# A gated-delta attention and SwiGLU kernel: chunk 0's K, its norms, its first scores, the first up products and the last stores cut into halves, with a new order of the whole program

## The chip, the cores and the metric

The kernel runs on one core of one Trainium2 chip. The metric is the device time of one execution in microseconds; a kernel's time is the median of its runs. TensorE is PE in the profile (its weight loads PEld), VectorE is DVE, ScalarE ACT, GpSimd POOL, and SyncE, whose queue issues nearly all DMAs, SP.

## The reference

Two stages follow each other, all in float32. The first is a delta rule over 768 steps for 4 batches and 8 heads of 48 columns. The second is a SwiGLU layer with RMS norm over the 3072 tokens, 384 columns wide and 1536 inside.

```python
k_n = k / (np.linalg.norm(k, axis=-1, keepdims=True) + 1e-06)
for t in range(S):
    kt, vt, bt = (k_n[:, :, t], v[:, :, t], beta[:, :, t, None])
    y[:, :, t] = np.einsum('bhd,bhde->bhe', q[:, :, t], state)
    v_old = np.einsum('bhde,bhd->bhe', state, kt)
    state = state + bt[:, :, :, None] * np.einsum('bhd,bhe->bhde', kt, vt - v_old)
...
rms = np.sqrt(np.mean(x * x, axis=-1, keepdims=True) + 1e-06)
xn = x / rms * rms_g
g = xn @ w_gate
silu = g * (1.0 / (1.0 + np.exp(-g)))
val = xn @ w_val
return (silu * val @ w_out).astype(np.float32)
```

Here x is y with the heads side by side, one row of 384 for each token.

## The kernel before

The 768 steps are cut into 12 chunks of 64 (`C`). In a chunk the recurrence becomes matrix work: the scores of K with K, the inverse of a unit triangular 64x64 matrix for each of 32 batch-heads, products of that inverse with V less what the state holds, scores of Q with K, and an update of the state. The 256 tokens of a chunk (4 batches of 64, kept as two token halves of 128) then go through the RMS norm and the feed-forward part.

Each chunk passes these stages:

- `load` reads K, Q and V; for chunk 0 K comes in two DMAs of 192 KB, one on SP's queue and one on ACT's. `norms` squares K on ACT (L711), sums on DVE (L712) and takes the root on POOL (L715). `turn` transposes K and Q on PE (L659) for the first chunks; later K goes through DRAM.
- `prep` makes the inverse. `scores` (L690) gives K with K, ACT scales it (L919), four DMAs store it to DRAM (`dkk`) and two read it back with the batch-heads on the partitions (`at`). DVE multiplies by beta (L938) and makes shares (L965, L975, L970), for chunks below 4; above, POOL does so. Then 15 steps of a product and a sum on DVE (L987, L993) build the inverse of 32x32 blocks. It goes out to DRAM (`dx`) and back into `mt` and `x2bd`, and three small products (L1044 or a DMA, L1068, L1092) merge the blocks to 64x64.
- `prep_first` does this for chunk 0 without DRAM: 16x16 blocks are copied out of the scores (L775, L777), turned on DVE (L779), scaled by the norms (L797, L800), run through 7 steps (L829, L835) and copied to `mtb` (L864, L866). A product with the rest of the scores gives `gmb` (L879, copies L889 and L891), and `recur` for chunk 0 applies it three times (L1225, L1240, copies L1254).
- `recur` otherwise takes the state into account (L1131, L1143), applies the inverse (L1192, copies L1277 and L1279), multiplies with the Q scores (L1206) and updates the state (L1291). For x it then squares on ACT (L1315), takes the mean on DVE (L1322) and the root on POOL (L1327), scales on ACT (L1333), transposes on PE (L1358) and multiplies by g (L1363 on DVE, L1367 on ACT).
- `ffn_plain` does the feed-forward part of chunks 0 and 1: up products of 128x256 (L1430), Silu (L1437), product (L1438), down products of 128x384 (L1412), first for six of the twelve blocks f of 128 inner columns, later for the rest. `ffn` does chunks 2 to 11 with fewer products: 15 instead of 18 for a half (L1523) and 7 instead of 8 in `down` (L1581, sums L1590).
- `weights` loads and converts the 18 weight tiles of 768 KB (ACT L617 and L618, DVE L619 and L620), which arrive as 64-bit floats in pairs of words.

No engine order is written out by hand. All operations go into a `Plan` with durations, priorities (`due`, `rush`) and dependencies. `settle` plans forward and backward `ROUNDS` times, and each number in `MOVES` seeds one further change that is replayed when the program is built (`vary`, `attempt`). The resulting order of each engine's instructions and of SP's DMAs is fixed. Up to a planned time `WARM`, `filler` puts products with the identity (L1701) into PE's planned gaps. Each engine runs its instructions in that order and waits for semaphores; SP uses eight DMA semaphores in turn.

The pieces that the change and the prediction touch are `load`, `turn`, `norms`, `prep_first`, the `fast` test in `prep`, the multiplication by g in `recur`, `up` in `ffn_plain`, and `add` and `store` in `down`. The stores of a chunk's result stand behind its last sums:

```python
def store(p):
    for bb in range(2):
        tok = (2 * bb + p) * S + c * C
        dma(out[tok : tok + C, :], o_sb[p][64 * bb : 64 * bb + 64], -1, ...)
```

## Time and profile before

| | us |
|---|---|
| median of 3 runs | 679.27 |
| the runs | 679.56, 673.34, 679.27 |
| the profiled execution | 678.64 |
| its span, first to last instruction | 676.3 |
| PE busy | 658.9 |
| DVE busy | 535.4 |
| ACT busy | 314.3 |
| POOL busy | 118.8 |
| mean granted PE clock | 0.997 |

A row of busy time by stretches has the stretch, its length, then for PE, PEld, DVE, ACT and POOL the busy time and in brackets the number of instructions, then PE's granted clock, the DMA share and GB/s. A row of the chain has start, length, and what the end waited for. A row of the timeline has start, length, engine, line, operation, output and inputs with sizes, the count, and in brackets the engine's idle time before it with what ended that. A float32 product of the program is two records of the trace.

### The profile page before, as it was taken

The numbers are of one execution on the slowest core, as the hardware profiler recorded it, in microseconds if no ns is written. First come the engines' busy times: TensorE is split into PE (matmuls) and PEld (weight loads), VectorE is DVE, ScalarE is ACT, GpSimd is POOL, SyncE is SP. The second block draws the span as 40 slices with busy tenths as digits, with TensorE's granted clock in tenths as the row PEclk, the third lists the DMA queues.
The fourth block names the chain that finished last, engine by engine and source line by source line (L and its number), as shares of the span: only waits on it lengthen the run. The fifth ranks groups of instructions, "written<-read, shape, count | busy, mean of one in ns | idle before, by whom it ended". The sixth has DMA issues, their size and how long they took to land.

```text
span 676.3 us, 23308 instructions
## 1 busy us (share of the span) xinstructions
PE 658.9 (97%) x9896; PEld 608.1 (90%) x9896; DVE 535.4 (79%) x1142; ACT 314.3 (46%) x763; POOL 118.8 (18%) x95
## 2 busy tenths in 40 slices
PE   8889989999998999999999999999999999999997
...
GB/s 95 155 257 80 191 205 143 270 90 128 92 121 125 43 75 121 104 66 135 82 74 116 84 103 119 97 44 106 122 46 91 102 75 48 25 57 2 25 1 23
DMA packets 285976, 66.61 MB, mean 98 GB/s; under 512 B 269104, under 2 KB 276784, under 8 KB 285872
## 3 DMA queue, kind: packets, MB, share of 16 engines
q1 hardware_dynamic: 284832, 64.93, 53.0%
q8 instruction: 77, 1.26, 0.8%
...
## 4 chain that ended last, share of the span: by engine, by line
PE 79%; DVE 8%; DMA 6%; SPq 4%; issue 1%; ACT 1%; POOL 0%; DVEq 0%
PE bank L1523 37%; PE bank L1581 21%; PE bank L1430 5%; SPq L509 4%; PE bank L690 3%; PE bank L1412 2%; DVE acc L993 2%; DMA at<-dkk 2%; PE bank L1206 2%; DVE acc L987 2%; DMA q<-in_q_dram 2%; PE bank L1092 1%; PE bank L1143 1%; PE bank L1192 1%; PE bank L1131 1%
## 5 line engine op out<-in xcount | busy, mean ns | idle before, releaser
L1523 PE MATMUL bank<-xf,w_in 128*128 128x128 f32 x1440 | 179.8, 277 | 0.0
L1523 PEld LDWEIGHTS bank<-xf,w_in 128*128 128x128 f32 x1440 | 170.0, 192 | 1.6 <-issue 0.8
L1534 DVE TENSOR_TENSOR tmp<-tmp,bank 128x512 f32<-128x512 f32 x180 | 120.7, 681 | 43.6 <-PE bank L1523 37.7
L1523 PE MATMUL bank<-xf,more 128*128 128x128 f32 x960 | 124.2, 277 | 0.0
L1523 PEld LDWEIGHTS bank<-xf,more 128*128 128x128 f32 x960 | 115.1, 192 | 1.3
L1536 ACT COPY tmp<-bank 128x512 f32<-128x512 f32 x120 | 69.6, 585 | 81.9 <-PE bank L1523 67.3
L1540 ACT ACTIVATE tmp<-tmp 128x256 f32<-128x256 f32 x120 | 49.7, 417 | 82.7 <-DVE tmp L1534 82.4
L993 DVE TENSOR_REDUCE acc<-acc 128x30 f32<-128x90 f32 (+4 forms) x165 | 78.0, 473 | 5.7
L1581 PE MATMUL bank<-wo_sb,hf 128*128 128x192 f32 x360 | 65.6, 333 | 0.6 <-DVE hf L1541 0.6
L938 POOL TENSOR_TENSOR at<-at,bs 128x1024 f32<-128x1024 f32 x8 | 18.9, 2360 | 246.9 <-DMA at<-dkk 148.1
L1581 PEld LDWEIGHTS bank<-wo_sb,hf 128*128 128x128 f32 x360 | 59.1, 193 | 2.1 <-DVE hf L1541 0.9
L987 DVE TENSOR_TENSOR acc<-acc,at 128x60 f32<-128x60 f32 (+4 forms) x165 | 56.4, 342 | 2.6
L1541 DVE TENSOR_TENSOR hf<-tmp 128x256 f32<-128x256 f32 x120 | 49.6, 429 | 10.4 <-ACT tmp L1540 9.2
L715 POOL TENSOR_TENSOR knrm<-ksum,half 128x16 f32<-128x16 f32 x12 | 35.7, 2971 | 88.3 <-DVE ksum L714 45.4
L1430 PE MATMUL bank<-xf,w_in 128*128 128x256 f32 x144 | 34.4, 385 | 0.3 <-DVE w_in L620 0.3
L1412 PE MATMUL bank<-wo_sb,hf 128*128 128x384 f32 x96 | 33.9, 493 | 0.0
L1430 PE MATMUL bank<-xp,w_in 128*128 128x256 f32 x144 | 33.1, 382 | 0.0
L1327 POOL TENSOR_TENSOR rs<-ms,mhalf 128x2 f32<-128x2 f32 (+1 forms) x13 | 9.7, 748 | 126.0 <-DVE ms L1322 85.6
L1430 PEld LDWEIGHTS bank<-xf,w_in 128*128 128x128 f32 x144 | 26.6, 190 | 5.6 <-DVE w_in L620 0.9
L1430 PEld LDWEIGHTS bank<-xp,w_in 128*128 128x128 f32 x144 | 27.0, 190 | 4.7 <-issue 0.2
L1590 DVE TENSOR_TENSOR tmp<-tmp,bank 128x192 f32<-128x192 f32 x30 | 10.5, 350 | 25.7 <-PE bank L1581 25.6
L1412 PEld LDWEIGHTS bank<-wo_sb,hf 128*128 128x128 f32 x96 | 17.8, 190 | 10.4 <-DVE hf L1438 0.6
...
## 6 DMA issues: line engine op xcount, KB each, us to landing
...
```

What stands on the lines that cost most here:

```text
L509: op = P.add(eng, dur, lambda: queue.dma_start(out=dst, in_=src), prio, r, w, lat=0.1)
L715: P.add("POOL", 2.95 if c < 2 else 3.3, lambda: nc.gpsimd.tensor_tensor(out=knrm[i2], in0=ksum[i2], in1=half, op=ALU.pow), pn, r=[("ksum", ...
L987: nc.vector.tensor_tensor(out=acc[:, 1:3, 0:n, j + 2 : W].rearrange("p a i t -> p i a t"), in0=acc[:, old, 0:n, j : j + 2, None].to_broadc ...
L993: nc.vector.tensor_reduce(out=acc[:, new, 0:n, j + 2 : W], in_=acc[:, lo : lo + 3, 0:n, j + 2 : W].rearrange("p a i t -> p i t a"), axis=A ...
L1412: nc.tensor.matmul(po[p].t[:, 0:DM], hf[:, spot(f), 128 * p : 128 * p + 128], wo_sb[:, spot(f)], start=(f == f0), stop=(f == f1 - 1), skip ...
L1430: nc.tensor.matmul(ps.t[:, TOK * side : TOK * side + TOK], w_in[:, side, h_, 3 * t + i_, n : n + 128], x_[:, 2 * t : 2 * t + 2].rearrange( ...
L1523: nc.tensor.matmul(g.t[:, 128 * z : 128 * z + 128], fac[:, side, 128 * f : 128 * f + 128], xf[:, xs], start=(begin and z == 0), stop=False ...
L1534: P.add("DVE", V(512), lambda t=t, g=g: nc.vector.tensor_tensor(out=t, in0=t, in1=g.t, op=ALU.add), -1, r=[g], w=[tk], last=g)
L1536: P.add("ACT", A(512), lambda t=t, g=g: nc.scalar.copy(t, g.t), -1, r=[g], w=[tk], last=g)
L1540: P.add("ACT", A(256), lambda t=t: nc.scalar.activation(out=t[:, 0:256], in_=t[:, 0:256], func=ACTF.Silu), -1, w=[tk])
L1541: P.add("DVE", V(256), lambda t=t, f0=f0, p=p: nc.vector.tensor_tensor(out=hf[:, spot(f0) : spot(f0) + 2, 128 * p : 128 * p + 128], in0=t[ ...
L1581: nc.tensor.matmul(g.t[:, 0:192], a_[:, f], b_[:, f], start=(begin and f == 0), stop=(f == 5), skip_group_check=True)
```

## The change

K of chunk 0 is loaded in four DMAs of 8 heads each, two on SP and two on ACT; its square, sum and turn work by such halves. The first scores are computed as 32x32 squares straight into two banks, and one copy for each bank replaces four. The up products of the first two blocks f are computed for 128 tokens at a time. For the last chunk each finished column half is stored at once, one DMA on SP and one on ACT. The scaling by beta and the shares go to POOL from chunk 2 on (`FASTC`), and all multiplications by g are done by ACT. The planner's constants, seed and list of moves are new, and the order of the instructions on every engine follows from them. The diff, with the lists of moves left out:

```diff
--- before.py
+++ after.py
@@ -22,42 +22,42 @@
 STRETCH = {"PE": 1.5, "ACT": 1.5, "DVE": 1.4, "POOL": 1.2, "SP": 1.0}
 ENGINES = ("PE", "ACT", "DVE", "POOL", "SP")
 OVERLAP = {"PE": 0.0, "ACT": 0.1, "DVE": 0.08, "POOL": 0.06, "SP": 0.0}
-ROUNDS, SEED = 24, 5
+ROUNDS, SEED = 24, 7
 MOVES = (
...
 )
-FETCH, AHEAD = 67.0, 160.0
+FETCH, AHEAD = 67.0, 120.0
 EARLY = 130.0
 FETCH0, AHEAD0 = 42.0, 130.0
-STICK = 2.0
+STICK = 0.5
 SHAKE = 0.06
 PATIENT = 0.3
 RING, LANES, FIRST, LAND = 2330, 8, 1.08, 0.9
-WARM = 60.0
-CLEAR = (0.3, 0.6, 0.9)
+FASTC = 2
+WARM = 56.0
+CLEAR = (0.2, 0.5, 0.8)
 TURNK = range(4, 12)
 BEGIN = 1.7
-ONSET = {"PE": 1.0, "ACT": 2.6, "DVE": 0.85, "POOL": 0.35, "SP": 0.5}
+ONSET = {"PE": 1.0, "ACT": 3.2, "DVE": 0.85, "POOL": 0.35, "SP": 0.5}
 TILE = 1.5
 EARLYM = 0.4
-MARGIN = 1.4
+MARGIN = 1.0
 TURNX = range(2, 11)
-DUE0 = 44.0
-DUE1 = 70.0
-DUE2 = 156.0
+DUE0 = 50.0
+DUE1 = 82.0
+DUE2 = 154.0
 PERIOD = 51.0
 W1 = 26.0
-CV2 = 75.0
-FAC = 105.0
+CV2 = 65.0
+FAC = 95.0
 TAIL0 = 20.0
-RUSH = 25.0
-RUSHW = 0.0
+RUSH = 35.0
+RUSHW = 10.0
 RUSH1 = 10.0
 RUSHC = 5.0
 
@@ -298,7 +298,7 @@
 
         rng = random.Random(n)
         kind, keys = rng.random(), list(keys)
-        a = rng.choice((rng.uniform(0.0, 650.0), rng.uniform(0.0, 220.0)))
+        a = rng.choice((rng.uniform(0.0, 650.0), rng.uniform(0.0, 220.0), rng.uniform(0.0, 110.0), rng.uniform(0.0, 110.0)))
         if kind < 0.25:
             w, s = rng.choice((10.0, 30.0, 80.0)), rng.choice((0.5, 2.0, 6.0))
             keys = [k + rng.gauss(0.0, s) if a < t < a + w else k for k, t in zip(keys, starts)]
@@ -638,9 +638,15 @@
             for g in range(2):
                 if key[0] not in what or key == "q2" and c > 1:
                     continue
+                if key == "k2" and c == 0:
+                    for hv in range(2):
+                        dst = t[64 * g : 64 * g + 64, 8 * hv : 8 * hv + 8, 0:D]
+                        s = src.rearrange("b (y g) t e -> g t (b y) e", g=2)[g, t0 : t0 + C, 8 * hv : 8 * hv + 8]
+                        dma(dst, s, pr + 0.1 * hv, w=[("k2", 0, g) if hv else ("k2h", g)], dur=0.7, work=0.75, desc=512, eng="ACT" if g else "SP")
+                    continue
                 dst = t[64 * g : 64 * g + 64, :, 0:D]
                 s = src.rearrange("b (y g) t e -> g t (b y) e", g=2)[g, t0 : t0 + C]
-                dma(dst, s, pr, w=[(key, c % NK, g)] if key == "k2" else q2k[8 * g : 8 * g + 8], dur=0.7, work=1.5 if c < 3 else 1.15, desc=1024, eng="ACT" if c == 0 and g and key == "k2" else "SP", bulk=c > 0 or key == "q2")
+                dma(dst, s, pr, w=[(key, c % NK, g)] + [("k2h", g)] * (c % NK == 0) if key == "k2" else q2k[8 * g : 8 * g + 8], dur=0.7, work=1.5 if c < 3 else 1.15, desc=1024, eng="ACT" if c == 0 and g and key == "k2" else "SP", bulk=c > 0 or key == "q2")
         if "v" in what:
             for g in range(2 if c == 0 else 0):
                 s = v.rearrange("b (y g) t e -> g t (b y) e", g=2)[g, t0 : t0 + C]
@@ -662,7 +668,7 @@
                         ident,
                     )
 
-            P.add("PE", 0.55, tr, pr, r=r + ["ident"], w=[ps, keys[hv]], ps=ps, size=8)
+            P.add("PE", 0.55, tr, pr, r=(r if isinstance(r, list) else r[hv]) + ["ident"], w=[ps, keys[hv]], ps=ps, size=8)
             if dst is qt:
                 out_ = dst[:, 4 * hv : 4 * hv + 4]
                 src_ = lambda ps=ps: ps.t.rearrange("p (u t) -> p u t", u=4)
@@ -701,17 +707,22 @@
         return [("kt", i, hv) for hv in range(2)] + [("ktr", i, n) for n in range(4)]
 
     def kkeys_(c):
-        return [("k2", c % NK, 0), ("k2", c % NK, 1)]
+        return [("k2", c % NK, 0), ("k2", c % NK, 1)] + [("k2h", 0), ("k2h", 1)] * (c == 0)
 
     def norms(c):
         i2 = c % 2
         pn = ((1.0, 8.0)[c] if c < 2 else due(c, 130))
         kd = k2[c % NK][:, :, 0:D]
 
-        P.add("ACT", A(768), lambda: nc.scalar.square(r_, kd), pn, r=kkeys_(c), w=[("r", 0), ("r", 1)])
-        P.add("DVE", V(768), lambda: nc.vector.tensor_reduce(out=ksum[i2], in_=r_, axis=AXL.X, op=ALU.add), pn, r=[("r", 0), ("r", 1)], w=[("ksum", i2)], lat=0.05)
-
-        P.add("DVE", 0.17, lambda: nc.vector.tensor_scalar_max(ksum[i2], ksum[i2], 1e-30), pn, w=[("ksum", i2)])
+        for hv in range(2 if c == 0 else 1):
+            x_ = slice(8 * hv, 8 * hv + 8) if c == 0 else slice(0, 16)
+            n = 384 if c == 0 else 768
+            rk, ks = ([("r", hv)], ("ks", hv)) if c == 0 else ([("r", 0), ("r", 1)], ("ksum", i2))
+            kk_ = [("k2", 0, g) if hv else ("k2h", g) for g in range(2)] if c == 0 else kkeys_(c)
+            P.add("ACT", A(n), lambda x_=x_: nc.scalar.square(r_[:, x_], kd[:, x_]), pn, r=kk_, w=rk)
+            P.add("DVE", V(n), lambda x_=x_: nc.vector.tensor_reduce(out=ksum[i2][:, x_], in_=r_[:, x_], axis=AXL.X, op=ALU.add), pn, r=rk, w=[ks], lat=0.05)
+
+        P.add("DVE", 0.17, lambda: nc.vector.tensor_scalar_max(ksum[i2], ksum[i2], 1e-30), pn, r=[("ks", 0), ("ks", 1)] if c == 0 else [], w=[("ksum", i2)])
         P.add("POOL", 2.95 if c < 2 else 3.3, lambda: nc.gpsimd.tensor_tensor(out=knrm[i2], in0=ksum[i2], in1=half, op=ALU.pow), pn, r=[("ksum", i2), "half"], w=[("knrm", i2)])
 
         def inv():
@@ -764,18 +775,29 @@
 
     def prep_first():
         kn, ktk, kkeys = k2[0], ktkeys(0), kkeys_(0)
-        turn(kn, kt[0], ktk, kkeys + [("k2p", 0)], 0.0, True)
-        ps = scores(kt[0], kt[0], 0.0, ktk, [])
-        for q_ in range(4):
-            rows, cols = slice(W * q_, W * q_ + W), slice(W * (q_ % 2), W * (q_ % 2) + W)
-            for d in range(2):
-                dst = sq1[rows].rearrange("p (x n) -> p x n", n=W)[:, d:16:2]
-                src = lambda d=d, rows=rows, cols=cols, ps=ps: heads(ps[d])[rows, :, cols]
-                if d:
-                    P.add("DVE", 0.45, lambda dst=dst, f=src: nc.vector.tensor_copy(out=dst, in_=f()), 0.0, r=[ps[d]], w=[("sq1", q_, d)], last=ps[d])
-                else:
-                    P.add("ACT", A(256), lambda dst=dst, f=src: nc.scalar.copy(dst, f()), 0.0, r=[ps[d]], w=[("sq1", q_, d)], last=ps[d])
-        sqk = [("sq1", q_, d) for q_ in range(4) for d in range(2)]
+        turn(kn, kt[0], ktk, ([("k2h", 0), ("k2h", 1), ("k2p", 0)], [("k2", 0, 0), ("k2", 0, 1), ("k2p", 0)]), 0.0, True)
+        pq = [Group(), Group()]
+
+        def squares():
+            for u in range(8):
+                for th in range(2):
+                    for d in range(2):
+                        for g in range(2):
+                            side = kt[0][64 * d : 64 * d + D, g, u, W * th : W * th + W]
+                            r0, n = 64 * g + W * th, W * u
+                            nc.tensor.matmul(pq[d].t[r0 : r0 + W, n : n + W], side, side)
+
+        P.rows = 32
+        P.add("PE", 1.7, squares, 0.0, r=ktk, w=pq, ps=pq, size=256)
+        P.rows = 128
+        for d in range(2):
+            dst = sq1.rearrange("p (x n) -> p x n", n=W)[:, d:16:2]
+            src = lambda d=d: pq[d].t[:, 0:256].rearrange("p (u n) -> p u n", n=W)
+            if d:
+                P.add("DVE", V(256), lambda dst=dst, f=src: nc.vector.tensor_copy(out=dst, in_=f()), 0.0, r=[pq[d]], w=[("sq1", d)], last=pq[d])
+            else:
+                P.add("ACT", A(256), lambda dst=dst, f=src: nc.scalar.copy(dst, f()), 0.0, r=[pq[d]], w=[("sq1", d)], last=pq[d])
+        sqk = [("sq1", d) for d in range(2)]
         P.add("DVE", 1.07, lambda: nc.vector.transpose(out=sq2, in_=sq1.rearrange("p (x h c) -> p c h x", h=2, c=16)), 0.0, r=sqk, w=["sq2"], port=1.0)
         turned = sq2.rearrange("p (j s) -> p j s", s=W)
         P.add("DVE", 0.35, lambda: nc.vector.tensor_scalar(out=at16, in0=turned[:, :, 0:16], scalar1=nh[:, 0:1], scalar2=None, op0=ALU.mult), 0.0, r=["sq2", "hm"], w=["at16"])
@@ -905,7 +927,7 @@
         kkeys = kkeys_(c)
         ktk = ktkeys(ikq)
 
-        fast = c < 4
+        fast = c < FASTC
         eng, e_ = (nc.vector, "DVE") if fast else (nc.gpsimd, "POOL")
         kkd = lambda d: [("kka", ikk // 2, d), ("kkb", ikk, d)]
         kkall = kkd(0) + kkd(1)
@@ -1359,11 +1381,6 @@
 
                 P.add("PE", 0.34, xtr, px, r=[("yn", p)], w=[psx, xkeys[p]], ps=psx, size=6)
                 for k_ in range(KT):
-                    if c < 2 and p:
-                        P.add("DVE", V(128), lambda p=p, psx=psx, k_=k_: nc.vector.tensor_scalar(
-                            out=xdst[:, 2 * k_ + p], in0=psx.t[:, 128 * k_ : 128 * k_ + 128], scalar1=g_sb[:, k_ : k_ + 1], scalar2=None, op0=ALU.mult
-                        ), pxv, r=[psx, "g"], w=[xkeys[p]], last=psx)
-                        continue
                     P.add("ACT", A(128), lambda p=p, psx=psx, k_=k_: nc.scalar.mul(
                         xdst[:, 2 * k_ + p], psx.t[:, 128 * k_ : 128 * k_ + 128], g_sb[:, k_ : k_ + 1]
                     ), pxv, r=[psx, "g"], w=[xkeys[p]], last=psx)
@@ -1423,16 +1440,21 @@
         def up(f):
             ps = Group()
             h_, i_, n = f // 6, f % 6 // 2, 128 * (f % 2)
-            for side, key in enumerate(("wg", "wv")):
-
-                def mm(side=side, ps=ps):
+            parts = ((0, 1),) if f > 1 else ((0,), (1,))
+            for tokens, (side, key) in itertools.product(parts, enumerate(("wg", "wv"))):
+                n0, n1 = 128 * tokens[0], 128 * tokens[-1] + 128
+
+                def mm(side=side, ps=ps, n0=n0, n1=n1):
                     for t in range(KT):
                         nc.tensor.matmul(
-                            ps.t[:, TOK * side : TOK * side + TOK], w_in[:, side, h_, 3 * t + i_, n : n + 128],
-                            x_[:, 2 * t : 2 * t + 2].rearrange("p a n -> p (a n)"), start=(t == 0), stop=(t == KT - 1)
+                            ps.t[:, TOK * side + n0 : TOK * side + n1], w_in[:, side, h_, 3 * t + i_, n : n + 128],
+                            x_[:, 2 * t : 2 * t + 2].rearrange("p a n -> p (a n)")[:, n0:n1], start=(t == 0), stop=(t == KT - 1)
                         )
 
-                P.add("PE", 1.33, mm, start + 3.9 * (f - f0), r=xk + [("wuse", h_)] + ready[(key, h_, i_)], w=[ps, (("sil", f % 2), ("hf", f, 0))[side]], ps=ps, size=12)
+                P.add(
+                    "PE", 1.33 * len(tokens) / 2, mm, start + 3.9 * (f - f0), r=[xk[p] for p in tokens] + [("wuse", h_)] + ready[(key, h_, i_)],
+                    w=[ps, (("sil", f % 2), ("hf", f, 0))[side]], ps=ps, size=12,
+                )
             a = f % 2
             P.add("ACT", A(256), lambda ps=ps: nc.scalar.activation(out=sil[a], in_=ps.t[:, 0:TOK], func=ACTF.Silu), -1, r=[ps], w=[("sil", a)], last=ps)
             P.add("DVE", V(256), lambda ps=ps: nc.vector.tensor_tensor(out=hf[:, spot(f)], in0=sil[a], in1=ps.t[:, TOK : 2 * TOK], op=ALU.mult), -1, r=[("sil", a), ps, ("tmp", 0)], w=[("hf", f, 0), ("hf", f, 1)] , last=ps)
@@ -1587,10 +1609,14 @@
 
         def add(p, n, t, g, r):
             dst = o_sb[p][:, 192 * n : 192 * n + 192]
-            P.add("DVE", V(192), lambda: nc.vector.tensor_tensor(out=dst, in0=t, in1=g.t[:, 0:192], op=ALU.add), -1, r=[g] + r, w=[("tmp", 3 + p)], last=g)
+            P.add("DVE", V(192), lambda: nc.vector.tensor_tensor(out=dst, in0=t, in1=g.t[:, 0:192], op=ALU.add), -1, r=[g] + r, w=[("tmp", 3 + p), ("oh", p, n)], last=g)
+            if c == NCH - 1:
+                for bb in range(2):
+                    tok = (2 * bb + p) * S + c * C
+                    dma(out[tok : tok + C, 192 * n : 192 * n + 192], dst[64 * bb : 64 * bb + 64], -1, r=[("oh", p, n)], w=[("out", c, p, bb, n)], desc=64, eng="ACT" if bb else "SP")
 
         def store(p):
-            for bb in range(2):
+            for bb in range(2 if c < NCH - 1 else 0):
                 tok = (2 * bb + p) * S + c * C
                 dma(out[tok : tok + C, :], o_sb[p][64 * bb : 64 * bb + 64], -1, r=[("tmp", 3 + p)], w=[("out", c, p, bb)], desc=64)
```

## Prediction

> **What bounds the kernel now.** I read the page first, then busy time by stretches, the chain of waits, and the timeline around each wait of PE.
>
> ```profile
> PE 658.9 (97%) x9896; PEld 608.1 (90%) x9896; DVE 535.4 (79%) x1142; ACT 314.3 (46%) x763; POOL 118.8 (18%) x95
> 40.00:50.00 10.00, 7.95 (x210) 6.75 (x209) 9.31 (x23) 6.00 (x16) 0.70 (x1) 1.00 0.81 214
> 70.00:80.00 10.00, 8.82 (x240) 6.72 (x240) 9.16 (x21) 4.23 (x7) 0.00 (x0) 1.00 0.85 215
> 80.00:90.00 10.00, 7.85 (x61) 6.14 (x51) 9.44 (x23) 8.18 (x23) 4.00 (x3) 1.00 0.89 216
> 300.00:350.00 50.00, 49.55 (x811) 47.71 (x810) 41.75 (x95) 23.59 (x60) 10.96 (x8) 1.00 0.54 95
> 219.00:220.00 1.00, 0.69 (x20) 0.57 (x24) 0.96 (x4) 0.00 (x0) 0.00 (x0) 0.68 0.41 63
> 220.00:222.00 2.00, 2.00 (x36) 1.83 (x29) 1.19 (x5) 0.39 (x1) 0.87 (x1) 0.50 0.42 66
> 222.00:224.00 2.00, 2.00 (x12) 2.00 (x11) 0.02 (x1) 0.00 (x0) 1.92 (x2) 0.81 0.28 30
> ```
>
> From about 91 us on PE is the bound (49.55 of 50 us in one stretch), with one exception: near 219 us it stops and then runs at a clock of 0.50. Before 56 us PE is filled with idle products on the identity (L1701); there DVE carries (9.3 of 10 us). The chain shows the turn from latency to work:
>
> ```profile
> 36.30 1.24 DVE at L938
> 49.56 0.55 PE bank L1358 x3
> 55.30 0.33 PE bank L1358 x3
> 56.51 2.59 PE bank L1430 x12
> ```
>
> The first product of chunk 0's gate weights (L1430) stands behind both token halves of x, whose turns (L1358) lie 5.7 us apart. In the timeline, where a bracket is the idle time before a row:
>
> ```profile
> 6.17 0.84 ACT L711 ACTIVATE r<-k 128x768 f32<-128x768 f32 x1 [0.26 <-DMA k<-in_k_dram]
> 9.30 5.95 POOL L715 TENSOR_TENSOR knrm<-ksum,half 128x16 f32<-128x16 f32 x2
> 16.38 0.36 DVE L800 TENSOR_TENSOR wo_sb<-wo_sb 128x256 f32<-128x256 f32 x1
> 27.90 0.87 DVE L864 COPY w_in<-wo_sb 32x512 f32<-32x512 f32 x2
> 78.41 1.15 PE L1206 MATMUL bank<-u,pt 64*64 64x48 f32 x64 [1.18 <-DVE u L1279]
> 86.60 0.87 PE L1358 MATMUL bank<-ident,yn 128*128 128x128 f32 x6 [2.15 <-ACT yn L1333]
> 91.19 1.46 PE L1430 MATMUL bank<-xp,w_in 128*128 128x256 f32 x6
> 219.31 0.49 PE L690 MATMUL bank<-qt,kt 48*64 48x64 f32 x8 [1.79 <-issue]
> 672.07 0.35 DVE L1590 TENSOR_TENSOR tmp<-tmp,bank 128x192 f32<-128x192 f32 x1 [1.26 <-PE bank L1581]
> ```
>
> Read: K lands at 6.17, its norms leave POOL about 12.2, the first block inverse is scaled at 16.4-16.7 and lies in place (L864) at 28.8. PE waits at 78 and 86 for chunk 1's recurrence; chunk 1's x feeds PE from 91.19 on.
>
> **The change, part by part.** The planner's numbers change too, so every queue is reordered; positions below are from the instruction order of the changed program.
>
> *K by halves.* The 192 KB loads of K land at 6.15 (two, on two queues), 9.08 (two) and 10.48, 1.46 us each. So the first half should be there at about 6.15 - 1.46 = 4.7, the second still at 6.15. Two issues more cost SP and ACT 0.4 to 0.7 us each (a K load takes SP 0.60); ACT's zeroing of the accumulators, 0.62 + 1.04, moves back by that and ends near 4.9, when the first half is there. The second square now stands behind ACT's table load (1.28 + 0.2): square 4.9-5.4, load to 6.9, square to 7.4, DVE sum to 7.95. POOL has one memset fewer (0.95) ahead of the root and is free at 8.2. The root starts at 8.2 instead of 9.3: -1.1.
>
> *Squares.* 64 matmuls are 128 records; by the 32x32 group of L1044 (64 in 1.04 us) they take 2.1 us, where L690 took 1.1. Two copies of 0.45 replace eight of 0.42 and 0.37: DVE does 0.45 instead of 1.7. But in the new order DVE's copy stands behind chunk 1's sum (0.95), which waits for K of chunk 1 (9.08), its square (0.84) and then 0.17: copy 11.15-11.6, scaled block 16.2 instead of 16.74. Only 0.5 is left of it here. Later the sum for chunk 2 (0.95 + 0.17, L712) has left the middle of this chain: spread at 24.4, inverse in place at 27.8: -1.0 against 28.8.
>
> *Recurrence of chunk 0.* gmb's copies (L889) ended at 34.95, behind a weight conversion of 1.99. They now stand ahead of it: 31.9, -3. Three rounds of copy (0.48) and 32 products (0.5), two halves interleaved, with ACT's weight work between them, put the last u at 39.4 instead of 46.2. DVE's means of squares (L1322) stand after 3 and 5 steps of chunk 1's inverse, at 43.3 and 45.2, instead of 47.8 and 51.6; then root 0.7, scaling 0.7, turn 0.4, three ACT copies of 0.3. With ACT's K copies and weights between (0.6, 0.93, 0.95), x's second half is there at 50.5.
>
> *Token halves.* In the built order both turns and the first product use the same bank, so the first half-product waits for the second half's copies all the same: I cost this part at nothing gained, and 24 products of 256 columns becoming 48 of 128 at 24 x (2 x 0.112 - 0.216) = +0.2. First up product: 51, against 56.3.
>
> *What that is worth at 91.* From 56.34 to 91.19 PE did 34.85 - 3.3 idle = 31.5 us of work: from 51 it is out of work at 82.5. Chunk 1's x sets the rest. DVE now does four weight conversions (1.5 us each) ahead of chunk 1's `at` product: it starts at 38.3 instead of 36.30, and with one conversion inside the inverse ends at 56.5 instead of 53.0: +3.5. Then the queue gives some back: in the old order four stores of chunk 2's scores (L509, 1.96 us from 56.86) stand between dx and its loads, in the new ahead of dx. dx goes out at 57.4, 10 loads of 0.48 and one weight load end near 67.5, the last lands 3 us later, so the state product (L1192) starts at 71-72 against 72.84. Chunk 2's scaling (L938, 1.23 + 1.1 + 0.7 + 0.3) leaves DVE for POOL, so u's copy (77.81) comes near 75.3 and the mean (83.12) near 80.4: x at 86 against 88.6. PE begins chunk 1 at 86.5 instead of 91.19: **-4.7**. Bounds: -8.7 (PE never waits: 51 + 31.5 = 82.5) and +3.5 (DVE's lateness at `at` goes through to x and nothing is given back). I take -4.7: its rows are those of this very chain. POOL's longer scaling (2.36 a product at L938) is hidden: chunk 2's mt is used at 127.4.
>
> *The stop at 219.* It lies in the only run of 192 short products (L1143, L1131, L690, L1068), after 152 of them; runs of 144 (at 163.7) and 128 show none. The new order's longest run has 160. The stop costs 1.8, the clock behind it 0.32 + 1.0 + 0.38 = 1.7: 24 products of L1581 took 5.08 instead of 3.9. Bounds: -3.5 (gone) and 0 (the run of 160 stops as well). As 160 lies just beyond 152, I take half: **-1.75**.
> The Trainium skill, page "TensorE: Matmul & The Clock Gate", section "Why this matters for your kernels", lets the clock fall only after an idle gap of over about 3 us. Here 1.79 us idle is followed by 0.50, and 2.15 us idle at 84.5 by 1.00, so the row decides; by that rule the clock's 1.7 would not belong to the stop, its half would be worth 0.9 and the sum 0.85 higher.
>
> *The end.* After the last sum (672.42) SP issues two stores, 0.59 each, the second at 673.0, landing 2.2 later. With one on SP and one on ACT the second waits for no first: **-0.6** (bounds -0.8 and 0).
>
> *Steady part.* The same products in a new order. PE's waits after 100 us, the stop aside, are 0.5, 0.3, 0.4 and 0.6: I leave them at 1.8, bounds 0 and 5.
>
> Sum against the profiled execution, 678.64 (span 676.3 and 2.3 around it): 678.64 - 4.7 - 1.75 - 0.6 + 0.2 = 671.8, taken as **672**. That execution is 0.6 below 679.27, the median of three (673.34 to 679.56).
>
> **Rivals.**
> A. *Chunk 1 takes the start's gain back.* PE begins chunk 1 at 91 as now: 678.6 - 1.75 - 0.6 = 676.3. For it: DVE's four conversions ahead of `at`. Against: 3.3 us of scaling moved from DVE to POOL behind it. The Trainium skill, page "DMA: Bandwidth & Descriptors", section "Rules for kernel authors", calls it useless to split a transfer in two, as both parts share the same engines. The trace agrees so far that the second half of K can't be there before 6.15, and this case is what the rule would make of the split.
> B. *Slower: `at` of chunk 1 arrives late.* In the new order a 768 KB weight load is issued on SP just ahead of the two `at` loads; now they stand behind `at`. A weight load lands 9.0 after its issue, `at` 6.5 after its own. Issued at 29.5 and served one after the other, `at` is there at 45 instead of 36.0. If the way from there to chunk 1's products stays as long as now (36.30 to 91.19, 54.9) and one conversion of 1.5 lies in it, they begin at 45.2 + 56.4 = 101.6, 10.4 later than now, and PE has nothing else to do: 678.6 + 10.4 - 2.35 = 686.7. It decides, on those terms, once the product starts past 37.2. Against: the queue moves 330 to 400 GB/s there (34 to 37 us), 2 us for a weight load.
> C. *All of it comes.* PE never waits ahead of chunk 1 (-8.7) and the stop is gone (-3.5): 678.6 - 8.7 - 3.5 - 0.6 = 665.8. For it: the waits at 78 and 86 are short and DVE has less to do. Against: DVE is 3.5 late at 56.
> D. *Nothing is given back, `at` in time.* 38.3 + 56.4 = 94.7, +3.5: 678.6 + 3.5 - 2.35 = 679.8. For it: chunk 1's chain has many steps on four queues. Against: the stores that leave its way on SP.
>
> **How the numbers follow.** My case (669 to 675) 0.48, A 0.17, B 0.08, C 0.13, D 0.14. About 1% is what measurements of this kernel can tell from no change: 672.5 and 686.1. Faster by over 1%: C's 0.13, 0.28 of mine (669 to 672.5 is 0.58 of it), 0.03 of A: 0.44. Slower: 0.05 of B and 0.01 of D: 0.06. Within: 0.50. The range 666 to 681 leaves out half of C, B and a little of D, 0.17 in all; my case's own is 669 to 675.
>
> **What would show it.** First gate product (L1449 in the new numbering) at 49 to 53; chunk 1's `at` product on DVE at 37 to 40; chunk 1's first up product at 84 to 89; no fall of the granted clock near 160 or 220 us; the last two stores on two queues, within 0.2 us. I am wrong if the first product comes after 55, if `at` waits for its DMA past 43, or if PE shows a new idle stretch of over 2 us behind 100 us.

## The result, and the profile after

The changed kernel takes 679.36 us (median of 20 runs, 674.46 to 681.55), the kernel before 675.96 in 20 runs beside them (673.18 to 679.56): ratio 1.0046, 95% interval 1.0029 to 1.0063. It is 0.5% slower; 672 had been forecast. The time lies inside the range that was stated (666 to 681), but on the side of the rival D (679.8), which had a chance of 0.14: a gain was forecast and a loss came. The execution of before that the prediction was summed on (678.64) lies 2.7 above that median, so on the median the same sum would have said 669.

Between the two profiled executions the span grows by 1.3, from 676.3 to 677.6; between the medians it is 3.4, as the profiled execution of before lies above its median. The table has us from the start of the span:

| | before | after | forecast |
|---|---|---|---|
| scaled block of chunk 0 (end of L800, now L822) | 16.7 | 20.1 | 16.2 |
| its inverse in place (end of L864, L886) | 28.8 | 29.1 | 27.8 |
| last copy of u in chunk 0 (end of L1254, L1276) | 46.2 | 46.8 | 39.4 |
| chunk 1's `at` product (L938, L960) | 36.30 | 42.57 | 38.3 |
| first gate product | 56.34 | 57.25 | 51 |
| chunk 1's first up product | 91.19 | 94.93 | 86.5 |
| last 12 products begin | 669.92 | 672.13 | |
| from there to the end | 6.4 | 5.5 | 0.6 less |

The page's lines of engines and of the queue q8, and busy time by stretches, whose columns are as in the profile before:

```profile
PE 660.8 (98%) x10006; PEld 609.6 (90%) x10006; DVE 530.2 (78%) x1126; ACT 314.1 (46%) x767; POOL 135.1 (20%) x105
...
q8 instruction: 78, 1.28, 0.9%
```

```profile
40.00:50.00 10.00, 7.26 (x243) 6.52 (x240) 7.92 (x19) 6.33 (x19) 1.75 (x3) 1.00 0.91 237
...
80.00:90.00 10.00, 8.12 (x174) 5.88 (x174) 7.79 (x15) 6.60 (x16) 0.82 (x1) 0.85 0.84 168
300.00:350.00 50.00, 48.70 (x800) 46.70 (x799) 37.91 (x84) 23.12 (x60) 10.43 (x8) 1.00 0.59 98
219.00:220.00 1.00, 1.00 (x8) 1.00 (x8) 1.00 (x2) 0.42 (x1) 0.00 (x0) 1.00 0.09 9
220.00:222.00 2.00, 2.00 (x82) 1.77 (x84) 1.93 (x6) 0.73 (x2) 0.00 (x0) 1.00 0.41 63
```

The stop at 219 is gone and the clock stays at 1.00 there: that step held. But PE is idle and slow in the start (granted clock 0.85 from 80 to 90). The chain of waits shows what stands on the way to the first gate product; "issue" is time in which PE waited for nothing that the profile shows:

```profile
28.66 0.43 DVE w_in L886
29.09 0.14 issue
29.22 3.48 PE bank L901 x64
32.70 1.85 PE bank L1262 x64
34.56 2.15 PE bank L1247 x12
36.70 1.06 PE bank L1262 x32
37.77 1.50 PE bank L1247 x8
39.27 2.93 PE bank L1262 x96
42.20 0.85 PE bank L1247 x4
43.05 1.18 PE bank L1262 x36
44.23 0.94 issue
...
47.85 0.35 PE bank L1313 x31
48.20 2.81 issue
51.01 0.58 PE bank L1313 x33
51.59 1.93 PE bank L1727 x8
53.52 0.34 PE bank L1380 x3
```

From 29 to 53 this chain never leaves PE: no copy of ACT stands in it, as the prediction had it, but PE's own products, two stops of 0.94 and 2.81, and 1.93 of fillers (L1727) in front of x's turn (L1380). A third stop follows in chunk 1, and more rows of the timeline explain what the start did not gain:

```profile
14.23 3.21 DVE L729 TENSOR_SCALAR knrm<-knrm 128x16 f32<-128x16 f32 x1 [0.20 <-POOL knrm L726]
...
17.96 1.70 DVE L819 TENSOR_TENSOR wo_sb<-w_in 128x256 f32<-128x256 f32 x1
...
37.40 0.56 DVE L619 TENSOR_SCALAR xf<-xf 128x768 uint32<-128x768 uint32 x1 [1.35 <-ACT xf L617]
...
41.70 0.96 DVE L620 CUSTOM_DVE_ANT_0 w_in<-more 128x1536 uint16<-128x1536 uint16 x1 [1.96 <-ACT more L618]
...
42.57 1.22 DVE L960 TENSOR_TENSOR at<-at,beta_b 128x1024 f32<-128x1024 f32 x1
...
57.25 3.01 PE L1449 MATMUL bank<-xf,w_in 128*128 128x128 f32 x25
...
85.77 0.56 PE L1228 MATMUL bank<-u,pt 64*64 64x48 f32 x21 [1.88 <-issue]
...
86.25 4.54 PE L1429 MATMUL bank<-wo_sb,hf 128*128 128x384 f32 x8
```

L729 (L718 before) took 0.13 for chunk 0 and 0.48 for chunk 1 in the kernel before, L819 (L797 before) 0.42. The eight records of L1429 behind the stop take 4.54; in an execution without that stop (chunk 1's scores moved, below) they took 2.85.

### The profile page after: what moved, and what is told of

It reads as the page before. It is cut to its first block, busy times and chain, and to the rows that moved or that the text cites. A ratio compares the mean times of both kernels' runs of the same rounds, so it can differ in the third digit from the quotient of the medians.

```text
span 677.6 us, 23529 instructions
## 1 busy us (share of the span) xinstructions
PE 660.8 (98%) x10006; PEld 609.6 (90%) x10006; DVE 530.2 (78%) x1126; ACT 314.1 (46%) x767; POOL 135.1 (20%) x105
## 3 DMA queue, kind: packets, MB, share of 16 engines
q8 instruction: 78, 1.28, 0.9%
## 4 chain that ended last, share of the span: by engine, by line
PE 85%; DVE 4%; DMA 3%; SPq 3%; ACT 2%; issue 2%; POOL 1%; POOLq 0%; ACTq 0%
PE bank L1545 39%; PE bank L1603 19%; PE bank L1449 7%; PE bank L1429 4%; PE bank L696 3%; SPq L509 3%; PE bank L1228 2%; PE bank L1214 2%; PE bank L1114 1%; PE bank L1165 1%; PE bank L1262 1%; PE bank L1313 1%; PE bank L1153 1%; PE bank L1090 1%; DMA k<-in_k_dram 1%
## 5 line engine op out<-in xcount | busy, mean ns | idle before, releaser
L1545 PE MATMUL bank<-xf,w_in 128*128 128x128 f32 x1440 | 178.9, 276 | 0.0
L1545 PEld LDWEIGHTS bank<-xf,w_in 128*128 128x128 f32 x1440 | 169.2, 192 | 1.6 <-issue 0.2
L1545 PE MATMUL bank<-xf,more 128*128 128x128 f32 x960 | 123.5, 277 | 0.1
L1545 PEld LDWEIGHTS bank<-xf,more 128*128 128x128 f32 x960 | 114.8, 192 | 1.9 <-issue 0.8
L960 POOL TENSOR_TENSOR at<-at,bs 128x1024 f32<-128x1024 f32 x10 | 27.2, 2715 | 272.0 <-DMA at<-dkk 109.7
L1009 DVE TENSOR_TENSOR acc<-acc,at 128x60 f32<-128x60 f32 (+4 forms) x165 | 57.4, 348 | 18.7 <-POOL at L992 15.2
L1603 PEld LDWEIGHTS bank<-wo_sb,hf 128*128 128x128 f32 x360 | 57.9, 190 | 0.9 <-issue 0.4
L1429 PE MATMUL bank<-wo_sb,hf 128*128 128x384 f32 x96 | 36.0, 514 | 0.0
L1449 PE MATMUL bank<-xp,w_in 128*128 128x256 f32 (+1 forms) x168 | 34.9, 355 | 0.8 <-DVE hf L1460 0.7
L1449 PE MATMUL bank<-xf,w_in 128*128 128x256 f32 (+1 forms) x168 | 34.0, 353 | 0.0
L1449 PEld LDWEIGHTS bank<-xp,w_in 128*128 128x128 f32 x168 | 27.8, 190 | 6.1 <-DVE hf L1460 1.5
L1608 ACT COPY tmp<-bank 128x192 f32<-128x192 f32 x30 | 9.6, 320 | 43.2 <-PE bank L1603 43.1
```

The source lines that it names most:

```text
L960: eng.tensor_tensor(out=at_, in0=at_, in1=(bt if fast else bs)[:, None, :].to_broadcast([128, W, W]), op=ALU.mult)
L1009: nc.vector.tensor_tensor(out=acc[:, 1:3, 0:n, j + 2 : W].rearrange("p a i t -> p i a t"), in0=acc[:, old, 0:n, j : j + 2, None].to_broadc ...
L1429: nc.tensor.matmul(po[p].t[:, 0:DM], hf[:, spot(f), 128 * p : 128 * p + 128], wo_sb[:, spot(f)], start=(f == f0), stop=(f == f1 - 1), skip ...
L1449: nc.tensor.matmul(ps.t[:, TOK * side + n0 : TOK * side + n1], w_in[:, side, h_, 3 * t + i_, n : n + 128], x_[:, 2 * t : 2 * t + 2].rearra ...
L1545: nc.tensor.matmul(g.t[:, 128 * z : 128 * z + 128], fac[:, side, 128 * f : 128 * f + 128], xf[:, xs], start=(begin and z == 0), stop=False ...
L1603: nc.tensor.matmul(g.t[:, 0:192], a_[:, f], b_[:, f], start=(begin and f == 0), stop=(f == 5), skip_group_check=True)
```

## What stops PE: counting instructions

The lines of the three stops differ, but their places in PE's stream follow one rule. I counted PE's instructions in the trace, matmuls, weight loads and semaphores together. In the kernel before, "issue" stops stand at instruction 1473 (46.1 us) and 6593 (217.3), in the changed kernel at 1473 (44.0), 1729 (48.0) and 3009 (83.7): each count leaves the remainder 193 when it is divided by 256. Busy time between two restarts of the changed kernel shows it without counting, 127 matmuls and 128 weight loads (and one semaphore):

```profile
45.10:51.00 5.90, 3.04 (x127) 2.70 (x128) 5.49 (x17) 4.71 (x15) 1.37 (x2) 1.00 0.59 158
```

Queue q8 of the page (packets, MB, share of the DMA engines) carries 78 transfers, 1.28 MB or 16 KB each; 10006 matmuls and 10006 weight loads are a little over 78 times 256. So PE's instructions seem to come in blocks of 256, one transfer each. Each stop spans the landing of the transfer of the block that PE needs next:

| stop (idle, from instruction to instruction) | the block before lasted | transfer begins after its start | transfer | PE goes on after landing |
|---|---|---|---|---|
| before, 217.3: 2.0 | 1.88 | 1.19 | 1.19 | 1.51 |
| after, 44.0: 1.15 | 4.59 | 2.58 | 1.79 | 1.37 |
| after, 48.0: 3.0 | 2.83 | 3.08 | 1.42 | 1.35 |
| after, 83.7: 2.1 | 3.47 | 2.60 | 1.41 | 1.56 |

This table counts a stop from the start of one instruction to the start of the next; the idle times in brackets and below are 0.2 to 0.3 shorter.

So theory 1: PE's instructions come in blocks of 256, and PE can't go on before about 1.4 us after the next block has landed; a block that is used up sooner leaves PE standing. 128 short records at 0.017 are used up in 2.2. All 17 traces fit: if q8's transfers are put to the blocks in order, the first to the one that begins at count 449, PE crosses none of 1,315 borders earlier than 1.23 us after the landing. When a transfer is asked for the traces don't say. In the stops it begins after PE has started the block before, but over a third of all transfers begin earlier than that, and then even a quick block does no harm: in the changed kernel the block at 242.9 us is used up in 2.15 and PE doesn't stop, as the next block's transfer had begun at 241.6.

The rivals: theory 2, the queues of DVE and ACT carry the start, and stops only fill slack; theory 3, the prediction's own, that some 152 short products in a row stop PE; theory 4, for L729, that DVE waited for POOL's work on memory. The Trainium skill, page "Runtime: NRT & Kernel Launch", section "Instruction fetch mechanics", describes such blocks of 16 KiB and 256 instructions and a refill ahead of use, and calls the cost of a border mostly hidden. The traces agree: 35 of the 1,315 borders have a stop of over 0.5 us. But those 35 are up to 4 us long, and the changed kernel has 5.6 us of them in one execution.

## The experiments

All keep the planned order of the kernel that they start from, unless the edit moves it. Ratios are to the kernel before.

**The count moved by 84, 164 and 256.** Products with the identity that fill PE's gap ahead of 16 us are replaced by more and smaller ones:

```diff
+        if len(n) == 9:
+            n = n[1:]
+            for _ in range(22):
+                nc.tensor.matmul(warm[0:32, 0:32], ident[0:32, 0:32], ident[0:32, 0:32])
```

(for 164: n[2:] and 43 products; for 256: n[2:] and 66)

> The changed kernel with one filler product (4 instructions of PE) of the gap before 16 us replaced by 22 products of 32x32 (88 instructions), the order of all else kept: every later instruction of PE moves back by 84 in its stream, at no time. Theory 1 (PE's instructions come in blocks of 256, and PE stands where a block is used up before the next one is there; these stops and the clock falls behind them are what the change lost): the stops stand again at count 193 modulo 256, now at other work: about 1.7 us together at 42 to 47 us instead of 3.75, none at 84 instead of 1.9, so no clock fall at 87; perhaps a new one of up to 1.8 in the run of 160 short products near 172. Time 3 to 5 us below the changed kernel, ratio to before 0.998 to 1.001. Theory 2 (the queues of DVE and ACT carry the start, the stops only fill slack): stops move as said, time within 1 us of the changed kernel, ratio 1.004 to 1.006. Theory 3 (the stops belong to certain lines, as the prediction had it with its count of short products): they stay at the same products, nothing moves, ratio 1.0046.

> The same with two filler products replaced by 43 of 32x32: 164 instructions. Theory 1: stops of 1.3 at 45, about 1 at 51 and perhaps 0.8 near 63, none at 84; the run near 172 without one; all at count 193 modulo 256; time 2 to 4 us below the changed kernel, ratio 0.999 to 1.002. Theory 2: ratio 1.004 to 1.006. Theory 3: stops where they were.

> The changed kernel with two filler products replaced by 66 of 32x32: a shift by 256 instructions, one whole block. If the period is 256: the stops are back at the same products as in the changed kernel (about 1 at 44, 2 to 3.6 at 48, about 2 at 84 unless that run has lost its lead), at count 193 modulo 256, ratio 1.003 to 1.006, where shifts of 84 and 164 gave 1.001. If the gain of those was the shift as such: ratio 1.001 and less.

Measured: shift by 84 676.77 us, ratio 1.0010 (0.9994 to 1.0025); by 164 676.37, 1.0011 (0.9993 to 1.0029); by 256 682.22, 1.0096 (1.0065 to 1.0127). PE's waits for "issue" in the timeline, of the three in turn:

```profile
47.48 0.37 PE L1228 MATMUL bank<-u,pt 64*64 64x48 f32 x10 [1.65 <-issue]
```

```profile
47.17 0.44 PE L1228 MATMUL bank<-u,pt 64*64 64x48 f32 x14 [0.96 <-issue]
52.92 0.38 PE L665 MATMUL bank<-ident,k 128*128 128x128 f32 x2 [0.90 <-issue]
```

```profile
46.76 0.95 PE L1262 MATMUL bank<-u,w_in 64*64 64x48 f32 x25 [0.89 <-issue]
53.70 0.90 PE L1313 MATMUL bank<-u,k 64*48 64x48 f32 x33 [3.90 <-issue]
```

With 84 and 164 the stops stand at other products, each again at count 193 modulo 256, and none is left at 84 us; with 256, one whole block, the first two are back at the very products of the changed kernel (x25 of L1262, x33 of L1313); the third, at 84, is not. Theory 3 falls, and theory 2 for the stops: a third or two thirds of a block of idle instructions takes off 2.4 us or 0.35%.

The idle products were not free, though. With the shifts by 164 and 256, PE has a stop of 0.4 to 0.5 among them, and the clock is at half for 3.4 and 6.8 us there:

```profile
12.78 3.67 PE L1729 MATMUL bank<-ident 32*32 32x32 f32 x66 [0.46 <-issue]
...
32.27 2.08 PE L901 MATMUL bank<-w_in,kk 64*64 64x64 f32 x64 [0.16 <-DVE w_in L886]
```

With 256 (these rows) gmb's products begin 3.0 later than in the changed kernel (29.22), and the stop at 49.6 was 3.9, so the ratio came out above the 1.003 to 1.006 that was expected; this run shows the period of 256, not the price of the stops. In the profiles with 84, PE has the recurrence's first products (L1262) 0.8 earlier than in the changed kernel and chunk 1's first product 3.1 earlier; with 164 it is 0.0 and 2.0. So most of the gain comes behind 32 us, where the stops moved. A stop in the run of 160 short products near 172, thought possible for 84, did not come: a block there is used up in 1.95, but the next one's transfer had begun 1.3 before it.

**The same in the kernel before.**

```diff
+        if len(n) == 11:
+            n = n[1:]
+            for _ in range(29):
+                nc.tensor.matmul(warm[0:32, 0:32], ident[0:32, 0:32], ident[0:32, 0:32])
```

> The kernel before, with one filler product ahead of 17.7 us replaced by 29 of 32x32: PE's later instructions move back by 112, the order of all else is kept. In the kernel before, the run of 192 short products (384 instructions) at 215 to 219 began just at the border of a block, so a whole block lay inside it; with 112 the border falls into its middle. Theory 1 (blocks): no stop there (1.8 to 2.0 gone) and no half clock behind it (1.7 gone), against small stops elsewhere in the start: 1.5 to 3.5 us lower, ratio 0.995 to 0.998. As the prediction had it (152 short products in a row stop PE wherever they stand): stop and clock fall stay, ratio 1.000.

Measured: 673.14, ratio 0.9961 (0.9943 to 0.9979). The run of 192 short products, in time stretches of the shifted kernel:

```profile
214.00:216.00 2.00, 2.00 (x142) 1.93 (x137) 1.58 (x4) 1.62 (x4) 0.00 (x0) 1.00 0.63 99
216.00:218.00 2.00, 2.00 (x43) 1.91 (x42) 1.93 (x7) 0.40 (x1) 0.00 (x0) 1.00 0.83 214
218.00:220.00 2.00, 2.00 (x14) 2.00 (x13) 2.00 (x8) 0.00 (x0) 0.43 (x1) 1.00 0.56 89
```

The same 192 products pass without a stop, as the border now lies inside the run, and the clock stays at 1.00. What the prediction put on the length of the run is the place of its border and the time of the next block's transfer. The gain of 0.4% is not that stop alone: the one at 46.1 is gone too (0.6), and a new one of 1.4 stands at 25.4. Nor is the stop at 217 the same in each execution: in the profile of the stores alone, below, which has the same count, its transfer began 0.78 after the block before (1.19 in before), the stop was 0.9 instead of 1.8, and no half clock followed.

**Less work for PE in chunk 0's recurrence.**

```diff
-                        gu.t[:, 192 * bb : 192 * bb + 192], ident,
-                        vt[:, 8 * bb + 4 * p : 8 * bb + 4 * p + 4].rearrange("s y e -> s (y e)"),
+                        gu.t[:, 192 * bb : 192 * bb + 48], ident,
+                        vt[:, 8 * bb + 4 * p],
...
-                                start=not k_, stop=True, skip_group_check=True,
+                                start=not k_ or y_ > 0, stop=True, skip_group_check=True,
```

> The changed kernel with the carry products of chunk 0's recurrence (L1247, 12 products, 24 records of 128x192 at 0.19 us) cut to 48 of their 192 columns, so V is left out of three quarters of chunk 0's corrections; the number of PE's instructions stays. It takes about 24 x (0.185 - 0.05) = 3.2 us of PE's work out of 34 to 43 us. If PE's work bounds the recurrence: the last copy of u (46.3) and the last short product (51.6) come about 3 earlier, first gate product near 54.3, ratio 1.000 to 1.003. If the blocks bound it (256 instructions for each 5.7 us there): the stops at 44 and 48 grow by what is saved, the last short product comes less than 1 earlier, ratio 1.004 to 1.005. If the copies on ACT bound it: PE shows new waits for ACT, less than 1 earlier.

This kernel leaves V out of three quarters of chunk 0's corrections. Measured: 679.16, ratio 1.0043 (1.0019 to 1.0067).

```profile
34.01 1.54 PE L1247 MATMUL bank<-vt,ident 128*128 128x48 f32 x12
...
36.55 1.09 PE L1247 MATMUL bank<-vt,ident 128*128 128x48 f32 x8
...
45.27 0.95 PE L1262 MATMUL bank<-u,w_in 64*64 64x48 f32 x25 [2.77 <-issue]
...
51.38 0.90 PE L1313 MATMUL bank<-u,k 64*48 64x48 f32 x33 [2.03 <-issue]
```

The carries took 1.54 and 1.09 instead of 2.22 and 1.57, 1.4 us less with the third group and not the 3.2 expected. All of it went into the stop at 44 (2.77 instead of 0.94): the restart is at 45.27 against 45.17. Blocks bound this stretch, not PE's work nor ACT's copies. The transfer behind that stop began at 42.23 (42.00 in the changed kernel) although PE had started the block before 1.45 earlier: here something else than PE sets when it begins. Behind the stops the clock was at half for three pieces (46.85 to 57.09), and the first gate product came at 60.12 instead of 57.25; the total is that of the changed kernel.

**Where the late blocks come from.** One weight load of SP's queue is held back (one entry moved in the order of its queue; in the second version it stands behind the output weights):

```diff
-SP: gate weights, g, value weights, V, output weights, K, K
+SP: gate weights, g, V, value weights, output weights, K, K
```

> The changed kernel with one 768 KB weight load (the value half of blocks 4 and 5, issued at 41.7 and not needed before 66) held back on SP's queue to just ahead of the next weight load, issued at 50.8; all else in order. Theory 1b (PE's block of instructions travels on the same DMA engines, and in the changed kernel stands behind the weights: at 45 the block's transfer began 3.1 us after the block before was begun, against 0.9 to 1.4 where the queues are quiet): the DMA engines are nearly empty from 45 to 50, the transfer begins 1 to 1.5 after, and the stop at 48 is 0.6 to 1.5 instead of 3.0. First gate product up to 2 earlier (55.3 to 56.5), time 0 to 2 us lower, ratio 1.002 to 1.0046. If the delay belongs to the short products alone: stop 3.0 as before, ratio 1.0046.

> The changed kernel with the weight load of 41.7 moved behind the next weight load and one K load on SP's queue, so that it can't be issued before 51 (in the earlier try it went out at 44.7, straight behind the V load, since nothing ahead of it waited). If the transfer of PE's block stands behind the weights: from about 46 to 51 the DMA engines are nearly idle, the block's transfer begins 0.9 to 1.7 after the block before was begun (3.1 in the changed kernel, 3.9 in the earlier try), the stop at 48 is 0.5 to 1.6 instead of 3.0. Ratio 1.000 to 1.004. If not: begin 3 after, stop 3, ratio 1.0046.

First version 678.78, ratio 1.0035 (1.0008 to 1.0062): nothing ahead of the load waited, so it went out at 44.7. The transfer of the block at 44 then began 1.95 after PE had started the block before (2.58 in the changed kernel) and the stop fell to 0.23; the next began 3.90 after (3.08) and its stop was 3.36. Second version, where the load went out at 50.15: 678.06, 1.0027 (0.9995 to 1.0059), begin 2.76, stop 2.53. The expected 0.9 to 1.7 did not come: other transfers kept the DMA engines at nine tenths or more until 47, and the block's transfer began at 46.8. Through the 35 stops of all runs, the four where the DMA engines were at most 0.67 busy between the start of the block before and the begin of the transfer had begins of 0.8 to 1.2; the 31 where they were full (0.97 and more) had 1.5 to 4.3. That the load is the cause stays likely and is not shown.

**DVE held by POOL.** The two zeroings (L568, L570) are given to ACT and placed where its queue is idle (the move in the order is not shown):

```diff
+    for n, t in ((13, m1bd.rearrange("p x a t -> p x (a t)")), (15, mt[0])):
+        P.ops[n].fn = lambda t=t: nc.scalar.copy(t, zero[:, 0:1, None].to_broadcast([128, 16, C]))
```

> The changed kernel with the two zeroings (L568, L570, 0.96 each) that POOL does at 15.6 to 17.4 given to ACT, which is idle from 13.1 to 16.5. Theory 4 (DVE's small scaling L729 took 3.21 instead of 0.18 because POOL worked on the same memory port until 17.4): L729 is free at about 15.7, the scaled block (L822) ends near 17 to 18.5 instead of 20.1, the inverse of chunk 0 is in place (L886) at 25.5 to 27 instead of 28.2 to 29.1. If the start's chain then carries it on, first gate product at 55.5 instead of 57.25 and time 1 to 2 us lower, ratio 1.001 to 1.003; if PE's stop at 48 eats it (it starts from when the block before was begun), first product within 0.5 of 57.25, ratio 1.004 to 1.006. If the port is not the cause, L729 still takes 3 us.

Measured: 680.07, ratio 1.0058 (1.0032 to 1.0085). This kernel's line numbers are 10 higher, L729 is L739, L822 L832, L886 L896:

```profile
14.22 1.43 DVE L739 TENSOR_SCALAR knrm<-knrm 128x16 f32<-128x16 f32 x1
...
17.90 0.42 DVE L832 TENSOR_TENSOR wo_sb<-wo_sb 128x256 f32<-128x256 f32 x1
...
26.35 0.85 DVE L896 COPY w_in<-wo_sb 32x512 f32<-32x512 f32 x2
```

Theory 4 holds: POOL worked from 14.16 to 17.42 in the changed kernel (1.48, 0.96 and 0.96 in a row) and now stops at 15.62; L729, which began at 14.2 in both, ends at 17.44 and at 15.65. All behind it comes 1.8 earlier. The Trainium skill, page "SBUF — State Buffer", section "Who interferes with whom", has it that one operation of DVE and one of GpSimd on their shared port shut each other out; the trace agrees. But nothing of the 1.8 arrived: the Q load was late in this execution (PE waited 3.2 for it until 25.6), gmb's products began at 30.74 instead of 29.22, and the stop at 48 was 3.6.

**Chunk 1's scores ahead of the last conversion; no fillers ahead of x's turn.**

```diff
-DVE: ... L619, L620, L960, L987, L997, L992 ...
+DVE: ... L960, L987, L997, L992, L619, L620 ...
```

```diff
+        if n == [4, 2, 1, 1]:
+            n = []
+            for _ in range(4):
+                nc.tensor.matmul(warm[0:32, 0:32], ident[0:32, 0:32], ident[0:32, 0:32])
```

> The changed kernel with the four DVE operations on chunk 1's scores (product with beta L960 and the three shares) put ahead of the last weight conversion (L619, L620) that stood before them; all else in the same order. Their data lands at 38.3 to 38.9. Theory 2 (chunk 1's chain, late by 6.3 at L960, sets its first up product): L960 starts at 39.3 instead of 42.6, chunk 1's inverse ends 3.3 earlier, its state product near 77 instead of 80, its first up product 2 to 3 earlier than 94.9; time 2 to 3 us lower, ratio 1.000 to 1.002. Theory 1 (stops alone): PE's stops stay as they are, time within 1 us, ratio 1.003 to 1.006.

> The changed kernel with the four filler products ahead of chunk 0's first turn of x (8 records of 128x512 and smaller, 2.0 us at 51.5 in the changed kernel) replaced by four of 32x32, which keeps the count of PE's instructions and so the blocks. They were planned into a gap that the stop at 48 has already taken. If they stand on the way to the first gate product: that comes 1.5 to 2.0 earlier (55.3 to 55.7 instead of 57.25), the stops stay at the same count, time 0.5 to 1.5 us below the changed kernel, ratio 1.002 to 1.004. If x waits for something else (DVE's mean, ACT), the first product stays within 0.3 of 57.25 and the ratio at 1.0046. If the missing fillers let the clock fall ahead of the up products, they cost up to 1.7 and the ratio is 1.005 to 1.007.

Measured: 678.85, 1.0034 (1.0011 to 1.0057), and 678.07, 1.0037 (1.0016 to 1.0058). Neither can be told from 1.0046, so both miss the gain that was expected. In the first, `at` had landed only at 40.8, so L960 came 1.8 earlier, not 3.3, and the stop at 47.5 was 3.6; in the second the stop was 3.1 and two stretches of half clock followed it (50.4 to 57.2), so that the first gate product came at 58.9. Inconclusive, each by itself.

**The four mends together** (the shift by 84 and the last three edits), and with the weight load held back (first and second version):

> The changed kernel with four mends together: the shift by 84 instructions, no fillers ahead of chunk 0's turn of x, the two zeroings on ACT, and chunk 1's scores ahead of the last conversion on DVE. If the losses add up (2.6 of the shift as measured, 1 of the fillers, 0.5 of the scores, and 1 of the zeroings now that the stop at 48 no longer eats it): 674 to 675, ratio 0.995 to 0.999, first gate product at 53 to 54.5. If PE's own work in chunk 0's recurrence (32 to 47 us, where PE is never idle but for the stops) bounds the start: first product not before 55, 676 to 677, ratio 0.999 to 1.002.

> The changed kernel with all five mends: the shift by 84, no fillers ahead of chunk 0's turn of x, the zeroings on ACT, chunk 1's scores ahead of the last conversion, and the weight load of 41.7 held back. If the stop that is left at 44 to 46 (2.0 in the version with four mends) stands behind the weights: it falls below 1, first gate product at 51.5 to 53, ratio 0.995 to 0.998. If PE's own work bounds that stretch: 53 as with four mends, ratio 0.998.

> The same with the four mends (shift by 84, fillers, zeroings, chunk 1's scores). If the stop of 2.0 that is left at 44 stands behind the weights it falls to under 1, the first gate product comes at 51.5 to 53, ratio 0.995 to 0.998. If the weight that is now late holds up the up products of blocks 4 and 5 (needed near 62): ratio 0.998 to 1.002 and a wait there.

Measured: four mends 674.91, ratio 0.9983 (0.9964 to 1.0002), first gate product 53.03; with the first weight move 674.51, 0.9969 (0.9946 to 0.9993), 55.66; with the second 675.88, 1.0006 (0.9979 to 1.0034), 52.69. So with the stops mostly out of the way the other losses seem to count, some 0.3% over the shift alone (the intervals just overlap), and the changed kernel is then about as fast as before. A stop of 1.3 to 2.3 at 43 to 46 stays in all three, against the under 1 that was expected with the weight load moved; the second version missed its 0.995 to 0.998.

**The stores alone**, in the kernel before, and with the shift by 112 (the old stores of the last chunk are dropped, which is not shown):

```diff
+                if c == NCH - 1:
+                    for bb in range(2):
+                        tok = (2 * bb + p) * S + c * C
+                        (nc.scalar if bb else nc.sync).dma_start(out=out[tok : tok + C, 192 * n : 192 * n + 192], in_=dst[64 * bb : 64 * bb + 64])
```

> The kernel before with the stores of the last chunk alone changed: each finished column half goes out at once, one DMA on SP's and one on ACT's queue. Prediction's step: the last two stores stand on two queues, the end comes 0.6 earlier (0 to 0.8), ratio 0.999; by the trace of the changed kernel, where from the start of the last 12 products to the end are 5.5 instead of 6.4, it is 0.9. If the two queues share what limits a store, nothing: 6.3 to 6.4 from the last 12 products to the end.

> The kernel before with the shift of PE's stream by 112 instructions and the last chunk's column halves stored at once on two queues. If both gains stand side by side: 0.4% of the shift and 0.6 to 0.9 us of the stores, ratio 0.994 to 0.996, 5.5 to 5.6 from the last 12 products to the end. If the stores gain nothing: 0.996 and 6.3.

Measured: stores alone 677.10, ratio 1.0008 (0.9987 to 1.0029), with 5.6 from the last 12 products to the end (667.70 to 673.3) where before had 6.4; with the shift 671.90, ratio 0.9929 (0.9903 to 0.9955), the fastest of all, 5.6 at its end too. The 0.8 at the end is seen in both profiles; in a total that scatters by 6 us from run to run it can't be told alone.

## Why the prediction was wrong, step by step

- *"K by halves": root at 8.2.* Right (8.41).
- *"Squares": scaled block at 16.2.* Wrong, 20.1. The products took 1.3 (2.1 had been taken) and the copy came at 11.0, as worked out; what failed is that the rows behind it were taken at the length they had in before. POOL, free earlier, did 3.3 us of work just then and held DVE's scaling of chunk 1's norms for 3.21 instead of 0.48 (shown by the zeroings on ACT), and L819, beside POOL's next operation, took 1.70 instead of 0.42: 4.0 together, about the 3.9 that was missed. Before's profile had such rows: L813, 128x128 elements, took 1.55 there and 0.40 now.
- *"Recurrence of chunk 0": last u at 39.4.* This is the step that sank the sum; it came at 46.8. From gmb's copies to the last u it took 13.3 (33.5 to 46.8) instead of 7.5, with only 0.94 of it idle on PE. The other 1.6 are gmb's copies, at 33.5 instead of 31.9: the inverse was 1.3 late, and gmb's products took 3.48 at a half clock that began at 28.94 (2.08 without it), which nothing in the sum had. The step added copies (0.48) and 32 products (0.5). Before's rows had 32 of those products at 1.13, carries of 1.57 between, and PE full from 35 to 45:

```profile
38.91 1.57 PE L1225 MATMUL bank<-vt,ident 128*128 128x192 f32 x8
40.41 1.13 PE L1240 MATMUL bank<-vt,w_in 64*64 64x48 f32 x32
...
35.00:40.00 5.00, 5.00 (x97) 4.67 (x94) 3.56 (x7) 2.83 (x5) 0.00 (x0) 1.00 1.04 381
40.00:45.00 5.00, 5.00 (x151) 4.51 (x152) 4.62 (x12) 3.74 (x11) 0.00 (x0) 1.00 0.79 226
```

So a chain of latencies was summed where the engine was full. In the changed kernel the blocks bound it beyond that: 1.4 us less work came back as stop.
- *"Token halves" nothing.* Both turns (L1380) did come ahead of the first product.
- *"What that is worth at 91": -4.7.* Its first term, a first product at 51, failed (57.25). Its second, `at` at 38.3, failed too (42.57): the four conversions ahead of it were counted by DVE's time alone, but two wait for ACT (1.35 and 1.96), whose queue holds them behind copies of u, which wait for PE. Chunk 1's state product came at 79.95, not 71 to 72: dx went out at 63.2 instead of 57.4, and the last of its loads at 75.6 instead of 67.5. From the first gate product at 57.25 to chunk 1's first at 94.93 PE stood for only 0.5 (for chunk 1's inverse, at 71) and 1.9 (the stop), and worked for 35.3, of which 1.7 is the half clock; before had 31.5. So PE's late start and its own work set chunk 1's beginning, not the late `at` alone. It came 3.7 later than before. D's +3.5 is close to that, and its 679.8 to the result, by luck: D had `at` at 38.3, the stop at 219 half gone and no new stops. The lateness of rival B was there, by DVE's queue instead of the DMA.
- *"The stop at 219": -1.75.* The stop and its half clock are gone, -3.5 against that profile, one bound of the step. Why it went was wrong: not 160 products instead of 192, but where the border of the block falls and when the next block lands. The same mechanism makes the three stops of the start (5.6 us in all, where the start of before had 0.6) and the half clock at 87 (1.7); no term of the sum had them.
- *"The end": -0.6.* Right in kind, 0.8 to 0.9 by the profiles, at or just past its bound of 0.8.
- *"Steady part": 0.* From chunk 2's first product (L1545, 187.36 against 182.95) to the last 12, the changed kernel is 2.2 shorter with the 3.5 of the stop in it: 1.3 lost, of it 0.9 more idle time from 300 to 350. Inside its bounds.

What does not show in single profiles: the same code ahead of 56 us put the first gate product at 56.34 in the profile of before and at 58.79 in that of the stores alone. Single times of the start are good to 2 or 3 us; the verdicts rest on the ratios.

What stays open: why the transfers of blocks begin 2 to 4 us late in the start, when they are asked for, and how the 0.3% of the mends divides among them.
